# A pad of 256 words instead of 16 behind the shifted weight words

## The chip, the cores and the metric

The kernel runs on one core of a Trainium2 chip. The metric is the device time of one execution in microseconds (us). The engines are named as in the profile: PE is TensorE (matmuls), PEld its loading of stationary operands, DVE is VectorE, ACT is ScalarE, POOL is GpSimd, SP is SyncE, which issues most transfers.

## What is computed

The reference is attention, then two dense layers with gates, one behind the other:

```python
# attention: 2 batches, 8 heads, 768 positions, head size 64
scores_l = scale * q @ k.T               # kept where |i - j| < 16
scores_s = scale * q @ k_sum.T + log(32) # k_sum: maximum of k over blocks of 32
a = softmax(concat(scores_l, scores_s))
x = a @ concat(v, v_sum)                 # v_sum: mean of v over blocks of 32
# x: 1536 tokens x 512
h = x @ w_in                             # 512 x 2048
x = (h * sigmoid(1.702 * h)) @ w_out     # layer 1
out = (sigmoid(x @ w_gate) * (x @ w_val)) @ w_out2   # layer 2, 512 x 1536
```

The weights of the layers come as 64-bit floating-point numbers and are read by the kernel as 32-bit words.

## The kernel before

**Numbers in two parts.** Each operand of the two layers is kept as a high part H and a low part L, both of type fp32r, and a product is made of three matmuls (`mm3`, line 171): L with H, H with L, H with H. All of them have a moving operand of 128x512 and a stationary slice of 128x128, and all are issued by line 176, so the profile shows them under this one line and tells them apart by their tiles.

**Layers.** There are three blocks of 512 tokens. A step is a group of 256 inner columns (8 groups in layer 1, 6 in layer 2) with one block. `first` (line 185) makes the inner values: in layer 1 two batches of 12 matmuls into ps_h; in layer 2 two of ps_h and two of ps_v. There the moving operand is a slice of x (xH, xL; in layer 2 the tiles yH and yL, which take the same places), and the stationary one a slice of 128 columns of a weight tile. ACT makes the sigmoid sg, DVE the product, ACT the high part gh, POOL the low part gl. `second` (line 220) multiplies these by the last weight matrix into ps_o, 24 matmuls per step, and DVE adds the result to acc (line 255). In layer 1 the moving operand of ps_o is a slice of gh or gl and the stationary one a slice of the weights; in layer 2 it is the other way round, with the weights moving. On TensorE the ps_o of a step stand behind or between the matmuls of the next step's `first`. The first four steps of layer 1 are set between the parts of attention.

**Weights.** `fetch` (line 145) transfers a piece of 256 columns or rows twice: into raw (2048 words per partition) and, shifted by 16 bits, into mid (2048 words and a pad). `decode` (line 92) makes wH and wL from both, on DVE and ACT, with scratch tiles da, db, dc. There is one raw and one mid, so the next piece is fetched when the last one has been read. The tiles of decoded weights are 12 (8 and, behind attention, 4 more).

**Where the tiles lie.** Tiles lie one behind another in each partition, in the order of their pools. From front to back, with bytes per partition:

| tiles | bytes each |
|---|---|
| ident | 512 |
| xH0 to xH2, xL0 to xL2 (later yH, yL) | 8192 |
| raw | 8192 |
| mid | 8192 + 64 |
| da, db, dc | 4096 |
| w: 8 tiles | 4096 |
| gh, gl | 4096 |
| sg: 2 tiles | 2048 |
| acc0, acc1 | 8192 |
| attention: vwin, mask, pick, warm, q, k, ks, kx, small ones, pt, e, vt, vm, vs | various |
| in the place of attention's, later: w (4 more), gh, gl, sg (2), acc2 | as above |

A slice of x, g or w as moving operand is 512 elements of 4 bytes in one piece and starts at a multiple of 2048 bytes from its tile's start. A stationary slice is 128 elements and starts at a multiple of 512 bytes from it.

Of the kernel before, what the change touches and what calls it, by code (L numbers as in the profile page):

```python
# [10 lines left out]
U32 = mybir.dt.uint32  # L11
# [6 lines left out]
P = 128  # L18
# [11 lines left out]
def attention_moe_moe2_kernel(ctx: ExitStack, tc: tile.TileContext, ins: dict, out: bass.AP):  # L30
# [26 lines left out]
    wraw = ctx.enter_context(tc.tile_pool(name="wraw", bufs=1))  # L57
# [87 lines left out]
    def fetch():  # L145

        if pieces:
            name, src, shifted = pieces.pop(0)
            n, m = src.shape[1], src.shape[2]
            raw = wraw.tile([P, n * m], U32, tag="raw", name=f"raw{name}")  # L150
            mid = wraw.tile([P, n * m + 16], U32, tag="mid", name=f"mid{name}")
            nc.sync.dma_start(out=raw.rearrange("p (a n) -> p a n", a=n), in_=src)
            to = mid.bitcast(U16)[:, 1:1 + 2 * n * m]
            nc.sync.dma_start(out=to.rearrange("p (a n) -> p a n", a=n), in_=shifted)
            raws.append((raw, mid, (P, n, m // 2)))

    def load_group(layer, g):
        tiles = weights[layer, g] = []
        ready[layer, g] = 0
        for i in range(len(mats[layer])):  # L160
            raw, mid, shape = raws.pop(0)
            hi, lo = (w_slots.tile(list(shape), F32R, f"w{layer}_{g}_{i}{x}") for x in "HL")
            tiles += [hi, lo]
            yield from decode(raw, mid, hi.rearrange("p a n -> p (a n)"), lo.rearrange("p a n -> p (a n)"))
            fetch()
            ready[layer, g] += 1
            yield
# [110 lines left out]
    with tc.manual_schedule(engines={mybir.EngineType.SP}), ExitStack() as es:  # L278
# [191 lines left out]
        sum_load(0, 3)  # L470
        load_q(4, nc.sync)
        fetch()
        make_identity(nc, ident)

# [143 lines left out]
```

## Time and profile before

| | |
|---|---|
| median of 3 runs | 676.21 us (676.18 to 676.91) |
| the profiled execution | 676.73 us |
| its span, first to last instruction | 675.0 us |
| mean granted clock of TensorE over the span | 0.986 of full speed |
| TensorE busy | 644.8 us, 96% of the span |
| VectorE busy | 417.9 us, 62% |
| ScalarE busy | 243.7 us, 36% |
| GpSimd busy | 167.5 us, 25% |

The profile is of one execution. Its own time is 1.7 us more than its span, which is what lies around the program's instructions. Busy times overlap between engines, and matmuls overlap each other: the next one starts before the one before has ended, so the distance between two starts is shorter than the duration of one.

### The profile page before, as it was taken

The numbers are of one execution on the slowest core, as the hardware profiler recorded it, in microseconds if no ns is written. First come the engines' busy times: TensorE is split into PE (matmuls) and PEld (weight loads), VectorE is DVE, ScalarE is ACT, GpSimd is POOL, SyncE is SP. The second block draws the span as 40 slices with busy tenths as digits, with TensorE's granted clock in tenths as the row PEclk, the third lists the DMA queues.
The fourth block names the chain that finished last, engine by engine and source line by source line (L and its number), as shares of the span: only waits on it lengthen the run. The fifth ranks groups of instructions, "written<-read, shape, count | busy, mean of one in ns | idle before, by whom it ended". The sixth has DMA issues, their size and how long they took to land.

```text
span 675.0 us, 8268 instructions
## 1 busy us (share of the span) xinstructions
PE 644.8 (96%) x3170; PEld 516.1 (76%) x3170; DVE 417.9 (62%) x628; ACT 243.7 (36%) x498; POOL 167.5 (25%) x164
## 2 busy tenths in 40 slices
PE   6677899999999999999999999999999999999997
PEld 4554677778888888888888888888888888888886
DVE  6797686459898777767678626427627627422223
ACT  3453765636443232333345425313213213211110
POOL 4453544313332221313131112111111111211110
PEclk9987799999999999999999999999999999999999
DMA  9978976007674242433333034324414413000013
GB/s 320 331 225 307 302 250 145 1 12 281 244 263 189 94 165 107 144 112 138 124 127 124 12 114 158 142 76 150 170 54 157 178 40 126 0 1 0 11 67 111
DMA packets 39672, 94.00 MB, mean 139 GB/s; under 512 B 2128, under 2 KB 2384, under 8 KB 39632
## 3 DMA queue, kind: packets, MB, share of 16 engines
q1 hardware_dynamic: 39056, 92.41, 39.7%
q10 hardware_dynamic: 576, 1.05, 0.4%
q8 instruction: 25, 0.41, 0.2%
q14 instruction: 15, 0.12, 0.0%
HBM read 88.74 MB, written 3.15 MB: 136 GB/s over the span
## 4 chain that ended last, share of the span: by engine, by line
PE 88%; DMA 3%; DVE 3%; ACT 3%; issue 1%; POOL 1%; SPq 0%; DVEq 0%; ACTq 0%; POOLq 0%
PE ps_h L176 35%; PE ps_o L176 34%; PE ps_v L176 15%; ACT e L389 2%; PE ps_s L375 2%; PE ps_x L424 2%; DMA raw<-in_moe_w_in 1%; PE ps_p L409 1%; DMA vt<-in_vt 1%; DMA k<-in_k 1%; ACT L389 1%; DVE dc L112 0%; PE ps_s L373 0%; DVE nm L380 0%; POOL gl L199 0%
## 5 line engine op out<-in xcount | busy, mean ns | idle before, releaser
L199 POOL TENSOR_TENSOR gl<-sg,gh 128x512 fp32r<-128x512 f32 x84 | 116.2, 1384 | 438.2 <-ACT gh L198 431.3
L255 DVE TENSOR_TENSOR acc<-ps_o,acc 128x512 f32<-128x512 f32 x143 | 96.5, 684 | 39.2 <-PE ps_o L176 39.0
L193 ACT ACTIVATE sg<-ps_h 128x512 f32<-128x512 f32 x84 | 49.9, 596 | 148.2 <-PE ps_h L176 148.2
L198 ACT CAST gh<-sg 128x512 fp32r<-128x512 f32 x84 | 52.1, 621 | 136.9 <-DVE sg L197 136.9
L197 DVE TENSOR_TENSOR sg<-ps_v,sg 128x512 f32<-128x512 f32 x36 | 24.8, 689 | 114.9 <-PE ps_v L176 113.2
L176 PE MATMUL ps_o<-gl,w_1H 128*128 128x512 f32 x192 | 75.9, 395 | 1.2 <-POOL gl L199 1.2
L176 PE MATMUL ps_h<-xH,w_0L 128*128 128x512 f32 x192 | 76.8, 404 | 0.0
L176 PE MATMUL ps_h<-xL,w_0H 128*128 128x512 f32 x192 | 76.6, 399 | 0.0
L176 PE MATMUL ps_h<-xH,w_0H 128*128 128x512 f32 x192 | 76.3, 397 | 0.0
L176 PE MATMUL ps_o<-gh,w_1L 128*128 128x512 f32 x192 | 75.7, 400 | 0.2 <-ACT gh L198 0.2
L176 PE MATMUL ps_o<-gh,w_1H 128*128 128x512 f32 x192 | 74.8, 390 | 0.0
L176 PE MATMUL ps_v<-yH,w_1L 128*128 128x512 f32 x144 | 56.8, 395 | 0.0
L176 PE MATMUL ps_v<-yH,w_1H 128*128 128x512 f32 x144 | 56.8, 395 | 0.0
L176 PE MATMUL ps_v<-yL,w_1H 128*128 128x512 f32 x144 | 56.8, 394 | 0.0
L176 PE MATMUL ps_h<-yH,w_0L 128*128 128x512 f32 x144 | 56.7, 394 | 0.0
L176 PE MATMUL ps_h<-yL,w_0H 128*128 128x512 f32 x144 | 56.7, 394 | 0.0
L176 PE MATMUL ps_h<-yH,w_0H 128*128 128x512 f32 x144 | 56.7, 394 | 0.0
L176 PE MATMUL ps_o<-w_2L,gh 128*128 128x512 f32 (+1 forms) x146 | 56.7, 388 | 0.0
L176 PE MATMUL ps_o<-w_2H,gh 128*128 128x512 f32 (+1 forms) x146 | 56.6, 387 | 0.0
L176 PE MATMUL ps_o<-w_2H,gl 128*128 128x512 f32 (+1 forms) x146 | 56.6, 387 | 0.0
L197 DVE TENSOR_TENSOR sg<-ps_h,sg 128x512 f32<-128x512 f32 x48 | 32.8, 685 | 32.6 <-ACT sg L193 32.6
L112 DVE SCALAR_TENSOR_TENSOR dc<-da,dc 128x1024 uint32<-128x1024 uint32 x34 | 49.6, 1459 | 0.5
(79 smaller groups left out, 1067.1 us busy)
## 6 DMA issues: line engine op xcount, KB each, us to landing
raw<-in_moe_w_out SPq DMA_DIRECT2D x14, 1024.0 KB, 5.0
mid<-in_moe_w_out SPq DMA_DIRECT2D x14, 1024.0 KB, 7.0
raw<-in_moe_w_in SPq DMA_DIRECT2D x8, 1024.0 KB, 5.5
mid<-in_moe_w_in SPq DMA_DIRECT2D x8, 1024.0 KB, 7.3
raw<-in_moe_w_gate SPq DMA_DIRECT2D x6, 1024.0 KB, 5.1
mid<-in_moe_w_gate SPq DMA_DIRECT2D x6, 1024.0 KB, 7.2
raw<-in_moe_w_val SPq DMA_DIRECT2D x6, 1024.0 KB, 5.1
mid<-in_moe_w_val SPq DMA_DIRECT2D x6, 1024.0 KB, 7.1
```

Source lines behind the costliest of these rows:

```text
L112: nc.vector.scalar_tensor_tensor(out=c, in0=a, scalar=0x80000000, in1=c, op0=ALU.bitwise_and, op1=ALU.bitwise_or)
L176: nc.tensor.matmul(ps, lhsT=a, rhs=b, start=i == 0, stop=i == n - 1)
L193: nc.scalar.activation(sg, ps, AF.Sigmoid, scale=1.702 if layer == 1 else 1.0)
L197: nc.vector.tensor_tensor(out=sg, in0=ps, in1=sg, op=ALU.mult)
L198: nc.scalar.copy(gh[:, f, :], sg)
L199: nc.gpsimd.tensor_tensor(out=gl[:, f, :], in0=sg, in1=gh[:, f, :], op=ALU.subtract)
L255: nc.vector.tensor_tensor(out=a[:, m, :], in0=ps, in1=a[:, m, :], op=ALU.add)
L375: nc.tensor.matmul(ps[:, j, :], lhsT=t[:, j, :], rhs=kt[:, j, :], start=False, stop=j == G - 1)
L389: nc.scalar.activation(e[:, j, :], s[:, j, :], AF.Exp, bias=nm[:, j:j + 1], scale=scale, accum_out=sm[:, j:j + 1])
L409: nc.tensor.transpose(ps[:, j, :], e[:, j, :], ident)
L424: nc.tensor.matmul(ps[64 * e:64 * e + 64, j, :], lhsT=vw(b, g * G + j)[:, h * D:(h + 1) * D], rhs=t[:, j, 64 * e:64 * e + 64], start=True, ...
```

## The change

The pad behind the words in mid is 256 words (1024 bytes) instead of 16 (64 bytes). mid then has 9216 bytes per partition instead of 8256, and every tile behind it lies 960 bytes further on. ident, x and raw stay where they are. The pad's words are not read by the matmuls, and `decode` reads mid[:, 0:2n] as before.

```diff
             raw = wraw.tile([P, n * m], U32, tag="raw", name=f"raw{name}")
-            mid = wraw.tile([P, n * m + 16], U32, tag="mid", name=f"mid{name}")
+            mid = wraw.tile([P, n * m + 256], U32, tag="mid", name=f"mid{name}")
             nc.sync.dma_start(out=raw.rearrange("p (a n) -> p a n", a=n), in_=src)
             to = mid.bitcast(U16)[:, 1:1 + 2 * n * m]
```

## Rows read from the trace of the kernel before

**Rows 1.** The page: busy time of TensorE, and the chain by line.

```profile
PE 644.8 (96%) x3170; PEld 516.1 (76%) x3170; DVE 417.9 (62%) x628; ACT 243.7 (36%) x498; POOL 167.5 (25%) x164
...
PE ps_h L176 35%; PE ps_o L176 34%; PE ps_v L176 15%; ACT e L389 2%; PE ps_s L375 2%; PE ps_x L424 2%; DMA raw<-in_moe_w_in 1%; PE ps_p L409 1%; DMA vt<-in_vt 1%; DMA k<-in_k 1%; ACT L389 1%; DVE dc L112 0%; PE ps_s L373 0%; DVE nm L380 0%; POOL gl L199 0%
```

**Rows 2.** Windows, 200 to 300 and 400 to 500 us.

```profile
core 0: us, PE busy (x) PEld busy (x) DVE busy (x) ACT busy (x) POOL busy (x), PEclk, DMA share, GB/s
...
200.00:300.00 100.00, 100.00 (x435) 81.32 (x434) 73.72 (x93) 33.61 (x49) 25.55 (x19) 1.00 0.37 132
...
400.00:500.00 100.00, 100.00 (x433) 80.85 (x432) 51.51 (x64) 30.92 (x44) 16.68 (x12) 1.00 0.35 126
```

**Rows 3.** Groups of line 176 by form, 149.3 to 675 us.

```profile
line engine op names shapes xcount | busy us, mean ns | idle before us <-releasers
...
L176 PE MATMUL ps_h<-xH,w_0H 128*128 128x512 f32 x160 | 63.0, 394 | 0.0
...
L176 PE MATMUL ps_o<-gh,w_1L 128*128 128x512 f32 x160 | 61.9, 390 | 0.0
L176 PE MATMUL ps_v<-yH,w_1L 128*128 128x512 f32 x144 | 56.8, 395 | 0.0
...
L176 PE MATMUL ps_h<-yH,w_0L 128*128 128x512 f32 x144 | 56.7, 394 | 0.0
...
L176 PE MATMUL ps_o<-w_2L,gh 128*128 128x512 f32 x142 | 55.6, 391 | 0.0
```

**Rows 4.** The chain in order of time: start us, us, what.

```profile
182.75 5.46 PE ps_o L176 x24
188.21 5.60 PE ps_h L176 x24
...
359.71 5.46 PE ps_o L176 x24
...
532.05 2.80 PE ps_h L176 x12
...
548.75 2.80 PE ps_h L176 x12
```

**Rows 5.** Timeline of PE, runs of layers 1 and 2: start us, us, what.

```profile
182.59 0.39 PE L176 MATMUL ps_o<-gh,w_1L 128*128 128x512 f32 x1
...
183.97 0.39 PE L176 MATMUL ps_o<-gh,w_1L 128*128 128x512 f32 x1
...
188.05 0.39 PE L176 MATMUL ps_h<-xH,w_0L 128*128 128x512 f32 x1
...
193.65 0.39 PE L176 MATMUL ps_o<-gh,w_1L 128*128 128x512 f32 x1
...
531.89 0.39 PE L176 MATMUL ps_h<-yH,w_0L 128*128 128x512 f32 x1
...
537.49 0.39 PE L176 MATMUL ps_o<-w_2H,gl 128*128 128x512 f32 x1
```

**Rows 6.** Timeline, a matmul and the loading beside it.

```profile
500.13 0.39 PE L176 MATMUL ps_h<-yL,w_0H 128*128 128x512 f32 x1
500.13 0.19 PEld L176 LDWEIGHTS ps_h<-yH,w_0H 128*128 128x128 f32 x1
```

**Rows 7.** Groups of PE by form, 0 to 149.3 us.

```profile
L409 PE MATMUL ps_p<-ident,e 128*128 128x128 f32 x96 | 16.9, 301 | 7.3 <-DVE pt L414 7.3
L176 PE MATMUL ps_h<-xH,w_0L 128*128 128x512 f32 x33 | 14.2, 452 | 0.0
...
L347 PE MATMUL ps_v<-ident,vm 128*32 128x128 f32 x16 | 4.4, 387 | 0.0
```

**Rows 8.** Waits of PE, 0 to 149.3 us: us in total, times, longest.

```profile
PE ps_s L373 <- ACT e L389: 11.1, 10, 2.5
PE ps_p L409 <- DVE pt L414: 7.3, 3, 3.1
```

**Rows 9.** The chain in order of time, its shares by line.

```profile
by line: PE ps_h L176 34.7%; PE ps_o L176 33.6%; PE ps_v L176 14.9%; ACT e L389 2.0%; PE ps_s L375 1.7%; PE ps_x L424 1.6%; DMA raw<-in_moe_w_in 1.5%; PE ps_p L409 1.1%; DMA vt<-in_vt 0.9%; issue 0.9%; DMA k<-in_k 0.7%; ACT L389 0.6%; DVE d
```

**Rows 10.** Waits of DVE, 190 to 400 us: us in total, times, longest.

```profile
DVE w_0L L119 <- PE ps_h L176: 4.3, 3, 1.4
```

## The prediction

> **What bounds the kernel now.** I read the page first. Its busy shares and its chain say the same thing: TensorE is busy 96% of the span, and ps_h, ps_o and ps_v (all three line 176) make 84% of the chain that ended last [rows 1]. [...]
>
> The chain in order of time shows layer 1 as runs of 24 matmuls that alternate. A run of ps_o takes 5.46 us, a run of ps_h 5.60 us; from 182.75 to 359.71 us there are 17 such runs of ps_o and 16 of ps_h between them, all at these two lengths [rows 4]. The two have the same shape, the same type, the same number of columns and one granted clock. The timeline makes it sharper [rows 5]. The ps_h run goes from 188.05 to 193.65: 5.60 / 24 = 233.3 ns per matmul. The ps_o run begins at 182.59; its first six matmuls take 1.38 us (230 ns each), and the other 18 take 188.05 - 183.97 = 4.08 us, 226.7 ns each. In layer 2 a ps_h batch with the ps_v batch behind it has 24 matmuls from 531.89 to 537.49, 233.3 ns again [rows 5]. So there are two rates, 226.7 and 233.3 ns, 6.6 ns (3%) apart.
>
> What goes with which rate? 233.3 ns belong to the matmuls whose moving operand is an x tile (xH, xL, and yH, yL in the same places). 226.7 ns belong to those whose moving operand is a g tile (layer 1) or a w tile (layer 2). It isn't the role of a tensor: in layer 1's ps_o g moves and w is stationary, in layer 2's ps_o w moves and g is stationary, and the means of the groups are 389 to 391 ns for both, against 394 and 395 for all the groups with x [rows 3]. What x alone has is its place. By the tile sizes in the program, the g and w tiles and the scratch tiles in front of them are whole multiples of 1024 bytes, so all g and w tiles begin at one address modulo 1024. The x tiles lie in front of the raw and mid tiles, and mid is 2064 words, 8256 bytes: 64 more than a multiple of 1024. So x begins 64 bytes lower, modulo 1024, than everything it is multiplied with. The stationary slice is 128 columns (512 bytes), so it starts at the tile's place or 512 bytes further on. The offset between moving and stationary start is thus 0 or 512 where the distance is 226.7 ns and 64 or 576 where it is 233.3 ns. I take this as the cause: the loading of the next stationary slice begins with the start of a matmul and runs beside it [rows 6], and the two readers get in each other's way more often at the one offset than at the other. That is an inference from two rates and two offsets; the rivals below live on what it leaves open.
>
> **The change, part by part.** It removes no instruction, adds none and moves none in time. mid becomes 2304 words, 9216 bytes = 9 x 1024, so every tile behind it lies 960 bytes further on, which is 64 less modulo 1024. Then x, g and w begin at one address modulo 1024, and the offset is 0 or 512 for all 128x512 matmuls of line 176. Where the offset theory holds:
>
> 1. *The x matmuls from 149.3 us on.* There are 3 x 160 + 3 x 144 of ps_h and 3 x 144 of ps_v, 1344 [rows 3], each with its pitch on the path. From 233.3 to 226.7 each: 1344 x (5.60/24 - 4.08/18) us = 1344 x 6.67 ns = 8.96 us. The lower end is the average of a whole ps_o run instead of its even part, (5.60 - 5.46) / 24 = 5.83 ns: 7.84 us.
> 2. *The starts of ps_o runs.* Layer 1: 5.46 - 24 x 0.22667 = 0.02 us per step. In layer 2 a step of 48 x matmuls and 24 of ps_o takes 548.75 - 532.05 = 16.70 us [rows 4]; 48 x 0.23333 = 11.20 leaves 5.50 for ps_o, 0.06 over. With 20 steps of layer 1 behind 149.3 us (480 / 24) and 18 of layer 2, that is 0.4 + 1.08 = 1.48 us. It stands directly behind x matmuls, so it may be the change from one rate to the other and go; it may also be the start of a run as such and stay. I take half, 0.74 us, with 0 and 1.48 as ends.
> 3. *The 96 ps_h before 149.3 us* (the groups there show 33, 32 and 32; one that reaches over the border is counted on both sides) [rows 7]. There attention sets the order, and TensorE waits for others: 11.1 us for the exponentials, 7.3 us for the copies of pt [rows 8]. I take nothing; if all were on the path, 96 x 6.67 ns = 0.64 us.
> 4. *The other operands.* kx with q, pt with vwin and mask with pick all lie behind mid and move together, so their offsets stay. Only ident lies in front: its offset to e in the transposes and to vm in the sums of v changes by 64 bytes. These are 96 and 16 [rows 7]; if each changed by 6.67 ns, 0.75 us either way. I take nothing, since the same waits stand around them.
> 5. *Transfers.* raw and x stay where they are, mid begins where it began, and its transfer has the same bytes. The tiles for q, k, v and vt begin elsewhere. On the chain are k with 0.7% and vt with 0.9% of 675.0 us [rows 9], 10.8 us; I take nothing, and if they changed by the 3% of the matmul rates, 0.3 us either way.
> 6. *What hides behind TensorE.* When TensorE gets 1.4% faster, the others must do a stage's work in 98.6 us instead of 100. VectorE has the most, 73.7 us [rows 2], so 25 us of cover remain. The weights are early too: in layer 1 the writes of decoded weights stood waiting for a tile still in use by ps_h, 4.3 us in three waits [rows 10]. The decoding waits for TensorE, not the reverse. So nothing takes the gain away.
>
> Sum: 8.96 + 0.74 = 9.70 us. The profiled execution took 676.73 us with a span of 675.0, so it would take 667.0. The median of the runs is 676.21, 0.52 lower; against it the forecast is 666.5 us.
>
> **The rivals.** *A: the place of the moving operand alone counts, and the kernel gets slower.* In the trace the matmuls at 233.3 ns differ from those at 226.7 ns both in their offset to the stationary slice and in where their own stream begins; no row has the one without the other. If a stream that begins where x begins costs time by itself, the change brings g and w to that place. The 3 x 160 and 3 x 142 ps_o from 149.3 us on [rows 3], 906 (one more reaches over the border), would then go from 226.7 to 233.3: + 6.04 us, less the change of rates of term 2 (0.74): 681.5 us. For it: the rate follows the moving operand whatever stationary slice is being loaded, the even or the odd one. Against it: a 64-byte shift of both streams leaves their relation as it is in the ps_o matmuls today, and I see no row in which a place by itself costs time. It decides if the ps_o runs of layer 1 go to 5.60 us.
>
> *B: the change doesn't do what it says.* The two rates come from something else that x has, such as the region of memory it lies in or groups of 12 accumulating matmuls instead of 6, and all stays at 676.2 us. For it: x tiles are six tiles in one stretch of memory. Against it: the ps_h and ps_v runs show one distance from the first matmul to the last, with no mark where a group of 12 ends, as 24 in 5.60 us says in layer 1 and in layer 2 [rows 4, 5]. [...]
>
> *C: part of it.* The rate of x falls to a value between the two, for instance because only one half of the stationary slices profits: 1344 / 2 x 6.67 ns = 4.5 us, 671.7 us. Against it: today both halves go at one rate, with x as with g and w.
>
> **How the numbers follow.** The offset theory 0.73, B 0.11, A 0.11, C 0.05. What a measurement of this kernel can tell from no change is about 0.2%, 1.35 us. The theory and C are faster by more, together 0.78; B is the same, 0.11; A is slower, 0.11. The likeliest case's own range takes all the open terms downward (8.96 + 1.48 + 0.64 + 0.75 + 0.3 = 12.1 us, 664.1) and upward (7.84 - 0.75 - 0.3 = 6.8 us, 669.4). Alone it holds about 0.7. To leave out no more than two in ten, the range has to take in C and B as well: 664.1 to 676.9, the highest of the runs before. A lies outside.
>
> **What the profile afterwards would show.** Right: in the chain, 24 ps_h in 5.44 us, as 24 ps_o; the groups of ps_h and ps_v at the mean of the ps_o groups; a layer 2 step in about 72 x 0.2267 = 16.32 us; TensorE still 100 us busy in each 100. Term 2 is right if the first six ps_o of a run also take 1.36 us. Wrong: ps_h runs at 5.60 still (B); ps_o runs at 5.60 too (A); ps_h at 5.44 but a wait of TensorE for gl, gh or the weights behind 180 us, which would show that term 6 was overlooked.

## The result and the profile after

The changed kernel takes 667.31 us, median of 4 runs (665.88 to 667.80), against 676.43 us for the kernel before in the same comparison (676.18 to 676.91, 4 runs). The ratio is 0.9861 with a 95% interval of 0.9843 to 0.9879: 1.4% faster. The profiled execution took 666.83 us with a span of 665.1, against 676.73 and 675.0. All five engines have the same instructions in the same order as before.

The page, busy times and the chain by line [rows 1]:

```profile
PE 632.1 (95%) x3170; PEld 515.6 (78%) x3170; DVE 419.3 (63%) x628; ACT 243.4 (37%) x498; POOL 167.1 (25%) x164
...
PE ps_o L176 33%; PE ps_h L176 33%; PE ps_v L176 15%; DMA mid<-in_moe_w_in 2%; DMA raw<-in_moe_w_out 1%; ACT e L389 1%; DMA vt<-in_vt 1%; PE ps_x L424 1%; DMA k<-in_k 1%; PE ps_s L375 1%; PE ps_p L409 1%; DVE pt L414 1%; DVE nm L380 1%; ACT L389 1%; DVE db L108 1%
```

TensorE has 12.7 us less of busy time and the others as much as before within 1.4 us. The windows that answer to [rows 2], with the same columns:

```profile
200.00:300.00 100.00, 100.00 (x443) 82.81 (x442) 75.45 (x94) 34.07 (x49) 25.32 (x19) 1.00 0.39 140
...
400.00:500.00 100.00, 100.00 (x443) 82.79 (x442) 52.94 (x66) 31.60 (x45) 16.77 (x13) 1.00 0.35 126
```

TensorE is still busy for all of each 100 us there, at the same granted clock of 1.00, so a stretch takes the number of its matmuls times the distance between two starts: 443 matmuls are counted in the 100 us where 435 and 433 were. The groups of line 176 by form, 149.3 us to the end [rows 3]:

```profile
L176 PE MATMUL ps_h<-xH,w_0H 128*128 128x512 f32 x160 | 62.2, 389 | 0.0
L176 PE MATMUL ps_o<-gh,w_1L 128*128 128x512 f32 x160 | 61.8, 389 | 0.0
...
L176 PE MATMUL ps_v<-yH,w_1L 128*128 128x512 f32 x144 | 56.0, 389 | 0.0
```

The groups with x had 394 and 395 and those of ps_o 390 and 391; now all have 389. The chain in order of time [rows 4]:

```profile
176.91 5.44 PE ps_h L176 x24
182.35 5.44 PE ps_o L176 x24
...
356.43 5.44 PE ps_o L176 x24
361.87 2.72 PE ps_h L176 x12
...
532.78 2.72 PE ps_h L176 x12
...
549.10 2.72 PE ps_h L176 x12
...
652.69 7.78 PE ps_o L176 x37
```

And the timeline of TensorE, for the run of ps_o and the run of ps_h that stand in [rows 5]:

```profile
182.19 0.39 PE L176 MATMUL ps_o<-gh,w_1L 128*128 128x512 f32 x1
...
183.55 0.39 PE L176 MATMUL ps_o<-gh,w_1L 128*128 128x512 f32 x1
...
187.63 0.39 PE L176 MATMUL ps_h<-xH,w_0L 128*128 128x512 f32 x1
...
193.07 0.39 PE L176 MATMUL ps_o<-gh,w_1L 128*128 128x512 f32 x1
```

The ps_h run takes 193.07 - 187.63 = 5.44 us instead of 5.60, 226.7 ns per matmul. The ps_o run takes 5.44 instead of 5.46, because its first six matmuls take 183.55 - 182.19 = 1.36 us instead of 1.38. There is one rate left, from the first matmul of a run to its last.

### The profile page after: what moved, and what is told of

The parts are those of the page before. It is cut to its first block, busy times and chain, and to the rows that moved or that the text cites. A ratio compares the mean times of both kernels' runs of the same rounds, so it can differ in the third digit from the quotient of the medians.

```text
span 665.1 us, 8268 instructions
## 1 busy us (share of the span) xinstructions
PE 632.1 (95%) x3170; PEld 515.6 (78%) x3170; DVE 419.3 (63%) x628; ACT 243.4 (37%) x498; POOL 167.1 (25%) x164
## 4 chain that ended last, share of the span: by engine, by line
PE 84%; DVE 6%; DMA 5%; ACT 3%; issue 1%; POOL 0%; SPq 0%; DVEq 0%; ACTq 0%
PE ps_o L176 33%; PE ps_h L176 33%; PE ps_v L176 15%; DMA mid<-in_moe_w_in 2%; DMA raw<-in_moe_w_out 1%; ACT e L389 1%; DMA vt<-in_vt 1%; PE ps_x L424 1%; DMA k<-in_k 1%; PE ps_s L375 1%; PE ps_p L409 1%; DVE pt L414 1%; DVE nm L380 1%; ACT L389 1%; DVE db L108 1%
```

## The experiments

Ratios are to the kernel before, run beside the experiment on one chip. Each pad kernel is one number changed in the line of the diff.

**Is it the offset, or where things lie?** Two kernels bring back the offset of 64 bytes in other ways. In the first, everything behind mid lies 64 bytes further on than in the changed kernel:

```diff
-            mid = wraw.tile([P, n * m + 256], U32, tag="mid", name=f"mid{name}")
+            mid = wraw.tile([P, n * m + 272], U32, tag="mid", name=f"mid{name}")
```

> The pad is 272 words, 16 more than in the changed kernel, so w and g begin 64 bytes further than x again, modulo 1024, while everything behind mid lies even 1024 bytes further from x than before the change. Offset theory: the runs of 24 ps_h go back from 5.44 to 5.60 us and the time to that of before, 676.4 us within 1. Rival (what counts is room between x and w, or where the tiles behind mid lie at large): 5.44 us and 667.3 us as in the changed kernel.

677.25 us, ratio 0.9992 (0.9977 to 1.0006). In the chain of this kernel the old lengths are back:

```profile
209.60 5.60 PE ps_h L176 x24
215.20 5.46 PE ps_o L176 x24
```

The second leaves w and g exactly where the changed kernel has them and moves x (its edit is against the kernel before):

```diff
-    ident = const.tile([P, P], F32, name="ident")
+    ident = const.tile([P, P + 240], F32, name="ident")[:, 0:P]
```

> The pad behind mid is the old one of 16 words, but the tile of ident in front of x is 960 bytes longer. All tiles behind mid then lie exactly where the changed kernel has them, x and raw lie 960 bytes further on too, and x is 64 bytes behind w and g again, modulo 1024. Offset theory: ps_h at 5.60 us per 24, ps_o at 5.46, time 676.4 us within 1. Rival (the place of w and g alone made them quick): w and g are in the new place, so 667.3 us.

677.12 us, ratio 0.9993 (0.9977 to 1.0008), and in its chain:

```profile
209.63 5.60 PE ps_h L176 x24
215.23 5.46 PE ps_o L176 x24
```

Both rivals fall. More room between x and w helps nothing, the new place of w and g helps nothing, and the offset of 64 bytes brings the 233.3 ns back each time.

**Does the sign count?** The pad is 240 words:

> The pad is 240 words, so w and g begin 64 bytes before x modulo 1024 instead of 64 behind it. Offset theory where only the distance counts: ps_h at 5.60 us per 24 and 676.4 us. Offset theory where the sign counts (the loading walks in one direction past the stream): ps_h at 5.44 us or at a third value, and a time between 667 and 676 us. Rival (only the very place of the change is good for x): slower than 676.4 us is possible, up to 681 us.

674.79 us, ratio 0.9948 (0.9930 to 0.9965). Its chain:

```profile
211.51 5.51 PE ps_h L176 x24
217.03 5.49 PE ps_o L176 x24
```

It does. With the stationary start 64 bytes before the moving one instead of behind it, a run of ps_h takes 5.51 us, a third value between the two. ps_o, whose own offset is untouched, takes 5.49, more than the 5.46 beside 233.3 ns: the length of a run depends on the runs beside it too.

**Which offsets are good?** Two kernels put the weight tiles of the changed kernel in pairs (H and L) at six offsets each, by gaps that are filled with zeros once (a few VectorE instructions more). The edit of the first, shortened at the marks; the other has 224, 288, 320, 352, 384 and 416 in its place, and in both the last two pairs follow behind attention:

```diff
-    pool([w_slots], 8, "w_a")
+    OFF = (32, 96, 128, 160, 192, 256)
...
+    def pair(i):
+        gap(OFF[i])
+        pool([w_slots], 2, f"w_{i}")
+
+    def gap(to):
+        n = (to - at[0]) % 512
...
+    for i in range(4):
+        pair(i)
+    gap(0)
```

> The twelve weight tiles are put, in pairs of H and L, at offsets of 32, 96, 128, 160, 192 and 256 bytes behind x, modulo 512, and g at 0, by gaps between the pairs. One look at the distance between starts for each offset. Offset theory: the ps_h and ps_v runs show different distances for different pairs, among them 226.7 and 233.3 ns, and the ps_o of one pair change in the same way; which offsets are the good ones is open, and if the period is 128 bytes, 128 and 256 give 226.7 ns and 192 gives 233.3. Rival (what counts is a start at a multiple of 128 bytes for the stationary operand alone): 226.7 ns for 128 and 256, 233.3 for all others.

In layer 1 three runs of ps_h or ps_o on end have one pair, so their length gives that pair's rate; the three differ by up to 0.02 us. From the chain of this kernel, the runs stand for 32, 96, 128, 160, 192 and 256 bytes, in this order:

```profile
216.42 5.60 PE ps_h L195 x24
222.02 5.62 PE ps_o L195 x24
...
250.07 5.58 PE ps_h L195 x24
255.65 5.60 PE ps_o L195 x24
...
283.54 5.49 PE ps_h L195 x24
...
299.98 5.45 PE ps_o L195 x24
```

> Like the first kernel with offset pairs, with 224, 288, 320, 352, 384 and 416 bytes. One look at the distance of starts for each. If the period of the offset theory is 256 bytes, as 256 gave the distance of 0 and 192 that of -64: 288 and 320 give 233.3 ns as 32 and 64 do, 384 gives 232 as 128, 224 gives 233.4 as -32, and 416 gives 233.4 as 160. If the period is 512: any value, with no tie to the half below.

From the chain of the second, the runs stand for 224, 288, 320, 352, 384 and 416 bytes:

```profile
216.77 5.60 PE ps_h L195 x24
222.37 5.59 PE ps_o L195 x24
...
250.35 5.60 PE ps_h L195 x24
255.95 5.62 PE ps_o L195 x24
...
284.00 5.58 PE ps_h L195 x24
...
300.75 5.60 PE ps_o L195 x24
```

The values of one half come again in the other: 32 and 288 have 5.60 and 5.59, 64 (the kernel before) and 320 both 5.60, 96 and 352 both 5.62, 128 and 384 both 5.58, 160 and 416 both 5.60, and 192 has 5.49 where 448 (the pad of 240 words) had 5.51. The period is 256 bytes, within 0.02 us. In the pad kernels x moves against all that lies behind mid, the tiles that other engines use included; here, modulo 512, the weight tiles alone move, and the length changes from pair to pair. A stationary start at a multiple of 128 bytes doesn't help by itself: 128 and 384 are among the costly offsets, with 5.58 us. These kernels took 684.17 and 686.84 us in one run each, but most of the excess lies ahead of the stretch that is read here: a run of 36 ps_h that begins at 149.41 us in the kernel before begins at 155.57 and 155.25 us in them, and why the time ahead of it is longer isn't shown. From there to the end of the spans (682.4 and 685.0 us) they take 526.83 and 529.75 us against 525.59: g and w stand at costly offsets too (ps_o runs of up to 5.62 us, against 5.46), as they never do in the kernel before.

**Is 256 as good as 0?** The pad is 64 words, 256 bytes:

> The pad is 64 words, so w and g begin 256 bytes behind x instead of at the same place, modulo 1024. If the offset theory's period is 256 bytes: ps_h at 226.7 to 229 ns, 24 of them in 5.44 to 5.50 us, and a time of 667.3 to 671 us, the lower end if 256 is as good as 0. If 0 and 512 are good alone: 5.60 us and 676.4 us. The one look at 256 gave 226.9 ns for ps_o and 229.0 for ps_v, in a kernel of mixed offsets, so the lower end is the likelier.

665.85 us, ratio 0.9825 (0.9803 to 0.9847), and one rate throughout:

```profile
198.01 5.44 PE ps_h L176 x24
203.45 5.44 PE ps_o L176 x24
```

So the change needs the starts to agree modulo 256 bytes (5.44 us per 24 at 256 as at 0), not modulo 1024. To see whether the smaller pad is even better, both ran side by side:

> The changed kernel once more, beside the one with a pad of 64 words on the same chip. Both have 226.7 ns for every 128x512 matmul in the looks so far, so if that is all that the pad does, the two ratios to the kernel before agree within 0.2%, near 0.985. If the smaller pad is better by more, as 0.9825 against 0.9861 in separate jobs would have it, something other than the matmul distances differs.

> The pad of 64 words again, beside the changed kernel: a ratio to the kernel before within 0.2% of that of the changed kernel, near 0.985. Rival: again some 0.3% lower than the changed kernel's.

The pad of 256 words gave 0.9857 (0.9833 to 0.9881), that of 64 words 0.9836 (0.9809 to 0.9863), with profiled spans of 666.2 and 666.4 us. The ratios are 0.2% apart, and the intervals overlap by more than half of their width: no difference can be told. The profiled executions show where the rest of the scatter lies. The run of 36 ps_h begins, and the time from there to the end of the span is, in us:

| kernel | offset of w behind x, bytes | run begins | from there to the end |
|---|---|---|---|
| before | 64 | 149.41 | 525.59 |
| pad of 272 words | 64 | 148.68 | 525.52 |
| ident longer | 64 | 148.72 | 525.58 |
| changed | 0 | 149.69 | 515.41 |
| changed, again | 0 | 150.88 | 515.32 |
| pad of 64 words | 256 | 149.03 | 515.37 |
| pad of 64 words, again | 256 | 151.04 | 515.36 |

Behind that run the kernels with the 64-byte offset agree within 0.1 us, and so do those with 0 and 256. The part ahead of it differs by up to 2.4 us among executions, and by 1.2 and 2.0 us between two executions of one kernel. The smaller pad does the same work with 768 bytes less per partition.

**How wide is the good place?** The x tiles get 128 words more, and their slices begin 124, 4 or 127 words in, by block; the pad of mid is 128 words, which keeps w and g at a multiple of 256 behind the x tiles. The first part of the edit, against the kernel before:

```diff
+    SHIFT = (124, 4, 127)
+
+    def x_tile(tag, name, blk):
+        t = xp.tile([P, KC * TB + 128], F32R, tag=tag, name=name)
+        k = SHIFT[blk]
+        return t[:, k:k + KC * TB].rearrange("p (k t) -> p k t", k=KC)
```

> w and g stay where the changed kernel has them; the x tiles are 512 bytes longer and their slices begin some words in, so that the stationary start lies 16 bytes behind the moving start in the first block of 512 tokens, 16 bytes before it in the second and 4 bytes behind it in the third. How wide is the good place at offset 0? Offset theory with a grain of 16 or 32 bytes: 4 behaves as 0 (226.7 ns), and 16 and -16 as 32 and -32 (233.3). With a grain of 64: all three at 226.7 or near. Lower than 226.7 in one of them would mean that the changed kernel is not yet at the best offset. Rival (a start at a multiple of 128 bytes counts, not the offset): all three at 233.

In the chain, one run of each of the three blocks, for 16, -16 and 4 bytes:

```profile
199.13 5.60 PE ps_h L183 x24
...
210.17 5.56 PE ps_h L183 x24
...
221.20 5.52 PE ps_h L183 x24
```

It is narrow. 16 bytes cost all of the 0.16 us, 16 bytes before cost 0.12, and even 4 bytes cost half of it, against each of the three grains that were expected. No offset tried is better than 0, with its 5.44 us. The kernel took 674.31 us in one run.

**Does the slice being loaded count, or the one in use?** Two kernels were to tell the slice being loaded from the slice in use. In the first the low weight tiles of the changed kernel alone move by 64 bytes (the edit is shortened):

```diff
+    def pairs(first, last):
+        for i in range(first, last):
+            pool([w_slots], 1, f"w_{i}H")
+            gap(64)
+            pool([w_slots], 1, f"w_{i}L")
+            gap(448)
```

> The high weight tiles lie at offset 0 to x and g, the low ones at 64. In a ps_h triple the order is low with xH, high with xL, high with xH, so one of the three next slices to be loaded is a low one, and one of the three slices in use is a low one. If it is the loading of the next slice that meets the stream: the distance after high with xH, beside which the next low slice is loaded, is 233.3 ns, the others 226.7; 24 ps_h take 5.49 us. If it is the slice in use: the distance after low with xH is 233.3 instead, with the same 5.49 us. Rival without offset: 5.44 or 5.60 us.

The chain, and the timeline of TensorE for one triple of this kernel:

```profile
205.85 5.55 PE ps_h L191 x24
```

```profile
205.69 0.40 PE L191 MATMUL ps_h<-xH,w_0L 128*128 128x512 f32 x1
205.93 0.39 PE L191 MATMUL ps_h<-xL,w_0H 128*128 128x512 f32 x1
...
206.16 0.39 PE L191 MATMUL ps_h<-xH,w_0H 128*128 128x512 f32 x1
...
206.38 0.40 PE L191 MATMUL ps_h<-xH,w_0L 128*128 128x512 f32 x1
```

On average over the triples of layer 1 from 180 us on, the distance behind low with xH is 235.9 ns, behind high with xL 228.3 and behind high with xH 229.1. The longest is where the shifted slice is in use, or one start after it was loaded; these can't be told apart here. The size fits neither reading: a run of 24 takes 5.55 us in the chain, not 5.49. (The kernel took 683.32 us in one run; its run of 36 ps_h begins at 155.93 us, as late as in the other kernels with gaps.) In the second the low x tiles of the changed kernel alone move:

```diff
+    def low_tile(name):
+        t = xp.tile([P, KC * TB + 128], F32R, tag="xL", name=name)
+        return t[:, 112:112 + KC * TB].rearrange("p (k t) -> p k t", k=KC)
```

> Only the low x tiles move, so that the stationary start is 64 bytes behind their start; xH, w and g stay at offset 0. In a ps_h triple (low with xH, high with xL, high with xH) only the second streams from a shifted tile. If the slice in use is what meets the stream: the longest distance is from high with xL to high with xH. If it is the loading of the next slice, seen one start later: the longest is from high with xH to low with xH. With the runs of the kernel that shifted the low weights, where the longest distance followed low with xH, the two can then be told apart. Either way 24 ps_h take 5.49 to 5.55 us, and ps_o stay at 5.44 to 5.46.

```profile
211.66 5.50 PE ps_h L181 x24
217.16 5.48 PE ps_o L181 x24
```

```profile
206.01 0.39 PE L181 MATMUL ps_o<-gh,w_1L 128*128 128x512 f32 x1
...
208.09 0.39 PE L181 MATMUL ps_o<-gh,w_1L 128*128 128x512 f32 x1
...
211.49 0.39 PE L181 MATMUL ps_h<-xH,w_0L 128*128 128x512 f32 x1
```

The sum is as expected for ps_h, but ps_o at 5.48 is longer than 5.44 to 5.46 although none of its operands moved. The excess lies at the start of the run, as the timeline of the run before shows: its first nine matmuls take 208.09 - 206.01 = 2.08 us (231 ns each), the other fifteen 3.40 us (226.7). On average over layer 1 from 180 us on, the distances of a ps_h triple are 229.8 ns behind low with xH, 230.1 behind high with xL and 228.2 behind high with xH. So the reading by the loading, seen one start later, fails, since it would have made the third the longest. The slice in use isn't shown either, since the first two are as good as equal. One hint is left, argued from two sums and tested by no run: the excess over 5.44 us is 0.11 with the low weights moved, about two thirds of 0.16, and 0.06 with the low x moved, about one third, as if it were enough that one of the two slices is off. The question stays open. (This kernel took 674.69 us in one run.)

## Why the prediction was right

**Step by step.** *The x matmuls from 149.3 us on* were worth what was said: 5.60 - 5.44 us per 24, 6.67 ns each, 8.96 us for 1344. *The starts of ps_o runs* were the mis-sized term. Half of 1.48 us was counted as going, and 1.22 went: 10.18 us in all, as worked out below, less 8.96. These lines of the chain, three of the kernel before and one of the changed one, and those shown above give it by parts:

```profile
149.41 8.40 PE ps_h L176 x36
...
365.17 2.80 PE ps_h L176 x12
...
662.57 7.80 PE ps_o L176 x37
```

```profile
149.69 8.18 PE ps_h L176 x36
```

Layer 1 comes out exactly: from the ps_o run at 182.75 to the start of layer 2 at 365.17 the kernel before took 182.42 us, and the changed one 361.87 - 182.35 = 179.52. That is 2.90 less, and 16 runs of 24 x 6.67 ns with 17 starts of 0.02 us make 2.56 + 0.34 = 2.90. From there to the last run of ps_o it was 297.40 us (662.57 - 365.17) and is 290.82, 6.58 less. With 864 x 6.67 ns = 5.76 for the x matmuls, 0.82 is left for the starts of 18 steps, 0.046 each where 0.06 had been read from one step. That the half was near enough is luck: it stood between two ends, and no row of before told which. The step that was sampled, 16.70 us, takes 549.10 - 532.78 = 16.32 now, as forecast.

*Before 149.3 us* nothing was counted, and no gain can be seen. The run of 36 ps_h that began at 149.41 us begins at 149.69. The waits that answer to [rows 8], and one more, have shifted among themselves:

```profile
PE ps_p L409 <- DVE pt L414: 9.7, 4, 4.2
PE ps_s L373 <- ACT e L389: 9.2, 9, 2.8
PE ps_x L424 <- DMA vwin<-vs: 2.7, 1, 2.7
```

The 0.28 us can't be put down to one of the open terms: the transposes had 301 ns in [rows 7] and show 284 now, the wait for vwin has 1.4 us more, and each comes from one execution. The changed kernel profiled again shows 312 ns for the transposes and begins the run at 150.88 us, so such values differ by more from one execution to the next, and no effect of the offset of ident can be seen. The sum closes. From that run to the end the kernel before took 675.0 - 149.41 = 525.59 us, the changed one 665.1 - 149.69 = 515.41: 10.18 less, and with 0.28 lost ahead of it 9.90, which is what the span and the profiled execution show. 9.70 was forecast. The medians differ by 9.12 us and the changed one is 667.31 where 666.5 was forecast; the 0.8 us between them are less than the part ahead of the run differs from one execution to the next.

*What hides behind TensorE* stayed hidden. From 180 us to the end TensorE shows no wait for another engine, VectorE's work in 200 to 300 us is 75.5 us, and the decoding waits for a weight tile in use almost as long as before [rows 10]:

```profile
DVE w_0L L119 <- PE ps_h L176: 4.0, 3, 1.3
```

**The rivals.** A, that the moving operand's place costs by itself, is refuted by the change: g and w moved to the place modulo 1024 that x had, and ps_o did not get longer (5.44 us per 24 instead of 5.46). B, that something else about x makes the two rates, is refuted by the change itself, which leaves x where it was and its groups of 12 as they were, and by the two kernels that bring the offset back (5.60 us per 24 in both). The runs show up to 7.5 ns per matmul (5.62 against 5.44 us for 24) that go with the starts of its two operands. C didn't happen here, but values between the two rates exist: 5.49 us at 192 bytes, 5.51 at -64, 5.52 at 4.

**What is argued only.** What the runs show is a cost that depends on an offset, with its sign (24 ps_h in 5.60 us at 64 bytes, 5.51 at -64) and with a period of 256 bytes (5.44 us at 0 and at 256). That the loading of a slice and the stream of the moving operand get in each other's way is the author's inference from this: no run shows it, and which of the two slices takes part is open. Nor is it shown why 226.7 ns are the least.

## What to carry to other kernels

Where TensorE is the bound, measure the distance between the starts of like matmuls, not their durations, and compare groups of one shape: two rates at one granted clock, as 226.7 and 233.3 ns at 1.00 here, can be a sign that places matter. Then work out where the operands start from the sizes of the tiles in front of them. A pad of 64 bytes that nobody reads put x off by 64 against its weights; here a pad that makes the starts agree modulo 256 bytes gave 1.4 to 1.8% of the whole kernel, and the smaller of the two cost 192 bytes per partition. So it can be tried to round the tiles in front of matmul operands up to 256 bytes, and to see whether all matmuls of a shape then have one rate. This was run for matmuls of 128x512 with operands of type fp32r and a new stationary slice for each; whether other types and shapes behave so is not shown.

## What the runs showed that was not expected

- The good offset is narrow: 24 matmuls take 5.44 us at 0 bytes, 5.52 at 4 and 5.60 at 16. Of the multiples of 32 that were tried only 0 and 256 have 5.44 to 5.46; 192 and 448 have 5.49 and 5.51, and all others 5.58 to 5.62.
- The sign counts: 64 bytes behind cost 0.16 us per 24, 64 bytes before 0.07.
- The length of a run goes with the runs beside it: ps_o at its own offset 0 took 5.44, 5.46, 5.48 or 5.49 us, by the offset of the ps_h around it. In the timelines shown the excess lies in its first matmuls: the first six in the kernel before, the first nine with the low x moved. Moving only the low weights cost 5.55 - 5.44 = 0.11 us per 24, twice the 0.05 that a third of 0.16 would be.
